# One score product per head and chunk, transposes on VectorE, and y on feature partitions in a gated linear recurrence with a dense block

## The chip, the cores and the metric

The kernel runs on one core of a Trainium2 chip. The metric is the device time of one execution in microseconds. The names used: PE is TensorE, DVE is VectorE, ACT is ScalarE, POOL is GpSimd, SP is SyncE, whose queue issues every DMA here.

## The reference

Inputs q, k, v and alpha have the shape 4 x 8 x 768 x 48 (batch, heads, tokens, features); q, k and v are normal numbers times 0.1, alpha is uniform between 0.8 and 1. The two weight matrices are float64, 384 x 2048 and 2048 x 384. What is computed:

```python
for t in range(S):
    state = alpha[:, :, t, :, None] * state + np.einsum('bhd,bhe->bhde', k[:, :, t], v[:, :, t])
    y[:, :, t] = np.einsum('bhd,bhde->bhe', q[:, :, t], state)
x = y.transpose(0, 2, 1, 3).reshape(B * S, H * D)      # 3072 x 384
h = x @ w_in
out = (h - np.tanh(h)) @ w_out                         # 3072 x 384
```

## The kernel before

The 3072 tokens are cut into 12 units of 256 tokens, a unit into two chunks of 128 (`CU`), three units to a batch entry. A unit goes through a recurrence (`gla`, lines 165 to 280) and a dense part (`moe`, lines 282 to 331). All arithmetic is fp32, and an fp32 matmul leaves two records in the trace (a transpose leaves one).

The recurrence. `load` fetches alpha, k, q and v with tokens on the partitions, two DMAs each per unit. `flip` (line 182) turns alpha, k and q round on PE, four 128 x 128 transposes per chunk and input, two heads in one (a head takes 64 partitions, 48 of them filled); the copies out of PSUM give `pre`, `kT` and `qT`. The scores of a chunk are built in seven levels of halving (line 204): at each level DVE multiplies q and k by products of alpha from and to the middle of a block (lines 209 and 213), PE makes 16 products of 64 rows, 128 columns of weights and 64 columns (line 220), DVE copies what a mask keeps into `scores` (line 225), and POOL extends the products of alpha (lines 234 and 235). The term of s = t is a row sum on POOL and DVE (lines 197 to 200). Then per chunk: y on token partitions from the state and from scores times v (lines 246 and 249), the sum with the diagonal term (253), three transposes that put features on the partitions (256), and, but for the last chunk of a batch entry, the update of the state through a transpose of k (265), a product (269) and POOL and DVE (278 and 279).

The dense part has eight steps (`FS`). `first` makes a PSUM tile of two 128-feature blocks by 256 tokens (line 292, 6 products), then four passes on ACT (square, tanh, a square of a polynomial, an overrun mask; lines 301 to 304) and six on DVE (305 to 310) that give g; where h h passes 0.25, h - tanh(h) is taken instead of the polynomial. `second` multiplies g by w_out (line 317, 4 products), two steps after its `first`.

The weights come as 28 blocks of float64 bits and are made fp32 by six passes on DVE, two on ACT and one on POOL (lines 124 to 135), through two buffers of `raw`. The temporary tiles of that conversion and of the dense passes share the tags u, z, t and w.

The order in which work is handed out is written at the end: the recurrence of a unit starts five steps before the dense part of the unit ahead of it, its 12 pieces spread over nine steps, its loads four steps earlier, and the weights before unit 0. Within that order a scheduler places each engine's instructions by their data. Each engine then runs in order.

Of the kernel before, what the change touches and what calls it, by code (L numbers as in the profile page):

```python
# [8 lines left out]
FP32 = mybir.dt.float32  # L9
# [17 lines left out]
ZK = C2 - ZB * ZB  # L27


@with_exitstack  # L30
def kernel(
# [12 lines left out]
    HD = H * D  # L44
    NP = H // 2
    G = CU * NP
    TU = CU * P
    UPB = S // TU
    NCH = S // P
    NU = B * UPB  # L50
    LEVELS = 7
    d_model, d_ff = moe_w_in.shape
    KT = d_model // P
    FT = d_ff // P
    FS = FT // 2

    w_in_r = moe_w_in.rearrange("(j p) f -> p j f", p=P)
    w_out_r = moe_w_out.rearrange("(j p) n -> p j n", p=P)
    out_r = out.rearrange("(t p) n -> t p n", p=P)

    consts = ctx.enter_context(tc.tile_pool(name="consts", bufs=1))
    two = ctx.enter_context(tc.tile_pool(name="two", bufs=2))
    three = ctx.enter_context(tc.tile_pool(name="three", bufs=3))
    ps_sc = ctx.enter_context(tc.tile_pool(name="ps_sc", bufs=2, space=PSUM))
    ps_tp = ctx.enter_context(tc.tile_pool(name="ps_tp", bufs=1, space=PSUM))
    ps_y = ctx.enter_context(tc.tile_pool(name="ps_y", bufs=1, space=PSUM))
    ps_h = ctx.enter_context(tc.tile_pool(name="ps_h", bufs=2, space=PSUM))
    ps_o = ctx.enter_context(tc.tile_pool(name="ps_o", bufs=1, space=PSUM))

    V, A, T, GP = nc.vector, nc.scalar, nc.tensor, nc.gpsimd  # L70

    ident = consts.tile([P, P], FP32, name="ident")
    make_identity(nc, ident)
    z_bias = consts.tile([P, 1], FP32, name="z_bias")
    V.memset(z_bias, ZB)
    m_bias = consts.tile([P, 1], FP32, name="m_bias")
    V.memset(m_bias, -U_MAX)
# [3 lines left out]
    mask = consts.tile([P, LEVELS, P // 2], FP32, name="mask")  # L81
    GP.memset(mask, 1.0)
    for l in range(LEVELS):
        L = 1 << l
        m = mask[:, l, :].rearrange("p (n j) -> p n j", j=L)
        n = P // (2 * L)
        GP.affine_select(out=m, in_=m, compare_op=ALU.is_ge, fill=0.0, base=0,
                         pattern=[[-2 * L, n], [0, L]], channel_multiplier=1)
        GP.affine_select(out=m, in_=m, compare_op=ALU.is_ge, fill=0.0, base=L - 1,
                         pattern=[[2 * L, n], [0, L]], channel_multiplier=-1)  # L90
# [3 lines left out]
    nat = [[consts.tile([P, CU, H, HP], FP32, name=f"{n}{i}") for n in ("an", "kn", "qn")]  # L94
           for i in range(2)]
    for i in range(2):
        for t in nat[i]:
            GP.memset(t[:, :, :, D:], 0.0)
    scores = [consts.tile([P, 2, G, P], FP32, name=f"scores{i}") for i in range(2)]
    for t in scores:  # L100
        V.memset(t, 0.0)
    states = [consts.tile([P, NP, 2 * D], FP32, name=f"state{i}") for i in range(2)]
    for t in states:
        GP.memset(t, 0.0)
# [4 lines left out]
    def load_w(dst, src):  # L109
        """A part of a weight matrix, of up to 512 columns: from float64 rounded to fp32, with  # L110
        what fp32 has no normal number for as 0 or infinite."""
        if moe_w_in.dtype == FP32:
            nc.sync.dma_start(out=dst, in_=src)
            return
        n = dst.shape[-1]
        raw = two.tile([P, 512], I64, name="raw")
        nc.sync.dma_start(out=raw[:, 0:n], in_=src)
        words = raw.bitcast(I32).rearrange("p (n w) -> p n w", w=2)
        lo, hi = words[:, 0:n, 0].bitcast(mybir.dt.uint32), words[:, 0:n, 1]
        e = two.tile([P, 512], I32, name="e", tag="u")[:, 0:n]  # L120
        m = two.tile([P, 512], I32, name="m", tag="z")[:, 0:n]
        low = two.tile([P, 512], FP32, name="low", tag="t")[:, 0:n]
        man = two.tile([P, 512], FP32, name="man", tag="w")[:, 0:n]
        V.tensor_scalar(out=e, in0=hi, scalar1=20, scalar2=0x7FF,  # L124
                        op0=ALU.logical_shift_right, op1=ALU.bitwise_and)
        V.tensor_scalar(out=e, in0=e, scalar1=896, scalar2=1151, op0=ALU.max, op1=ALU.min)
        V.tensor_scalar(out=e, in0=e, scalar1=23, scalar2=0x3FFFFFFF,  # L127
                        op0=ALU.logical_shift_left, op1=ALU.bitwise_and)
# [8 lines left out]
    def weights():  # L137
        """In the order in which the first unit needs them."""
        w = 512
        for i in range(d_ff // w):  # L140
            for j in range(KT):
                load_w(w_in[:, j, i * w:(i + 1) * w], w_in_r[:, j, i * w:(i + 1) * w])
# [236 lines left out]
```

## Time and profile before

| what | value |
|---|---|
| median of 3 runs | 1134.95 us (1134.72 to 1138.42) |
| profiled execution, span | 1140.3 us, 14741 instructions |
| PE busy | 1045.0 us, 92% |
| DVE busy | 805.0 us, 71% |
| ACT busy | 320.6 us, 28% |
| POOL busy | 342.8 us, 30% |
| mean granted PE clock | 0.909 |

The profile gives no other time for the profiled execution than its span, from the first to the last instruction; it is 5.4 us over the median of the runs. Busy times overlap between engines. [...]

### The profile page before, as it was taken

To read this page: it belongs to the slowest core of one execution; us is meant where nothing else is said; L and a number is where in the kernel's file an instruction comes from. 1 tells how busy PE (TensorE), PEld (TensorE's weight loads), DVE (VectorE), ACT (ScalarE), POOL (GpSimd) and SP (SyncE) were. 2 spreads that over 40 slices of the span, in tenths; PEclk is the share of its full clock that TensorE was granted. 3 is DMA by queue.
4 is the path that set the end of the run, shared out by engine and by line. 5 is a ranking of instruction groups with operands and counts; after the bars stand their busy time and mean duration, and the time that the engine had idled before them with its cause. 6 is when DMAs were issued, how large, how long until landed. Compare 5 with 4: busy or idle time off the path is not lost.

```text
span 1140.3 us, 14741 instructions
## 1 busy us (share of the span) xinstructions
PE 1045.0 (92%) x5752; PEld 845.6 (74%) x5752; DVE 805.0 (71%) x1212; ACT 320.6 (28%) x569; POOL 342.8 (30%) x293
## 2 busy tenths in 40 slices
PE   3765648999999999999999999999999999999988
PEld 2764548877877878778777788778787788777765
DVE  6688896584684677776774777685775676776766
ACT  2012330321421331421511431521502322413433
POOL 6454443043042044043132043143132152141000
PEclk9999755887998899989988999998979999989999
DMA  9433620110110020110200110200200000000000
GB/s 175 81 91 97 150 73 1 27 30 14 27 31 14 1 56 15 29 28 15 56 1 15 35 23 14 50 8 14 56 1 15 1 1 15 1 1 15 1 14 14
DMA packets 107396, 37.11 MB, mean 33 GB/s; under 512 B 100672, under 2 KB 103744, under 8 KB 107328
## 3 DMA queue, kind: packets, MB, share of 16 engines
q1 hardware_dynamic: 107328, 36.19, 14.1%
q8 instruction: 45, 0.74, 0.3%
q14 instruction: 23, 0.19, 0.1%
HBM read 31.46 MB, written 4.72 MB: 32 GB/s over the span
## 4 chain that ended last, share of the span: by engine, by line
PE 79%; DVE 15%; POOL 2%; issue 2%; ACT 1%; DMA 0%; SPq 0%; POOLq 0%; DVEq 0%
PE sc L220 24%; PE h L292 24%; PE o L317 20%; PE y L249 4%; DVE scores L225 3%; PE tp L185 2%; PE y L246 2%; PE up L269 2%; DVE e L129 1%; DVE W L209 1%; DVE z L307 1%; DVE e L127 1%; PE tp L265 1%; DVE m L131 1%; DVE e L124 1%
## 5 line engine op out<-in xcount | busy, mean ns | idle before, releaser
L220 PEld LDWEIGHTS sc<-W 64*128 64x128 f32 x2688 | 324.9, 217 | 92.7 <-issue 68.7
L220 PE MATMUL sc<-W 64*128 64x64 f32 x2688 | 338.1, 305 | 53.6 <-DVE W L213 41.0
L292 PE MATMUL h<-xT,w_in 128*128 128x256 f32 x1152 | 325.1, 426 | 5.1 <-DVE g L310 3.8
L317 PE MATMUL o<-w_out,g 128*128 128x384 f32 x768 | 278.7, 504 | 0.2 <-DVE g L310 0.2
L292 PEld LDWEIGHTS h<-xT,w_in 128*128 128x128 f32 x1152 | 231.7, 213 | 46.0 <-issue 4.8
L225 DVE COPY_PREDICATED scores<-mask,sc 128x512 f32<-128x512 int32 x168 | 147.8, 882 | 117.4 <-PE sc L220 115.1
L317 PEld LDWEIGHTS o<-w_out,g 128*128 128x128 f32 x768 | 147.5, 198 | 84.0 <-issue 7.7
L301 ACT ACTIVATE sq<-h 128x512 f32<-128x512 f32 x96 | 57.4, 598 | 440.9 <-PE h L292 437.1
L235 POOL TENSOR_TENSOR pre<-pre 128x512 f32<-128x512 f32 x84 | 118.3, 1409 | 115.5 <-DVE W L209 112.3
L234 POOL TENSOR_TENSOR suf<-suf,pre 128x512 f32<-128x512 f32 x72 | 100.3, 1393 | 140.3 <-DVE W L213 137.5
L305 DVE TENSOR_TENSOR w<-h,sq 128x512 f32<-128x512 f32 x96 | 66.2, 690 | 93.1 <-ACT th L302 92.4
L209 DVE TENSOR_TENSOR W<-qT,pre 128x512 f32<-128x512 f32 x84 | 60.1, 716 | 24.9 <-POOL pre L235 14.9
L310 DVE COPY_PREDICATED g<-large,h 128x512 f32<-128x512 int32 x96 | 70.6, 736 | 3.3
L309 DVE SCALAR_TENSOR_TENSOR g<-z,w 128x512 f32<-128x512 f32 x96 | 70.8, 737 | 1.8
L307 DVE SCALAR_TENSOR_TENSOR z<-z,sq 128x512 f32<-128x512 f32 x96 | 70.2, 731 | 0.0
L303 ACT ACTIVATE z<-sq,z_bias 128x512 f32<-128x512 f32 x96 | 69.6, 725 | 0.0
L304 ACT ACTIVATE large<-sq,m_bias 128x512 f32<-128x512 f32 x96 | 69.3, 722 | 0.0
L308 DVE SCALAR_TENSOR_TENSOR z<-z,sq 128x512 f32<-128x512 f32 x96 | 67.7, 705 | 1.9
L306 DVE TENSOR_TENSOR h<-h,th 128x512 f32<-128x512 f32 x96 | 66.7, 695 | 0.0
L213 DVE TENSOR_TENSOR W<-kT,suf 128x512 f32<-128x512 f32 x72 | 56.4, 784 | 14.2 <-POOL suf L234 14.2
L278 POOL TENSOR_TENSOR state<-state,pre 64x192 f32<-64x192 f32 x32 | 23.1, 722 | 139.3 <-DVE state L279 69.8
L249 PE MATMUL y<-vt,scores 128*128 128x48 f32 x384 | 53.2, 291 | 4.7 <-DVE scores L225 4.7
(60 smaller groups left out, 737.1 us busy)
## 6 DMA issues: line engine op xcount, KB each, us to landing
raw<-in_moe_w_in_dram SPq DMA_DIRECT2D x12, 512.0 KB, 3.9
raw<-in_moe_w_out_dram SPq DMA_DIRECT2D x16, 384.0 KB, 3.1
an<-in_alpha_dram SPq DMA_DIRECT2D x24, 192.0 KB, 3.3
kn<-in_k_dram SPq DMA_DIRECT2D x24, 192.0 KB, 3.5
qn<-in_q_dram SPq DMA_DIRECT2D x24, 192.0 KB, 3.1
vt<-in_v_dram SPq DMA_DIRECT2D x24, 192.0 KB, 3.9
out_dram<-ob SPq DMA_DIRECT2D x24, 192.0 KB, 1.9
```

Of the source, the lines that this page charges most:

```text
L209: V.tensor_mul(W1, q1, p1)
L220: T.matmul(sc[:, g, :], lhsT=Wf[rows, g, :], rhs=Wh[rows, g, :, 1, :], start=True, stop=True)
L225: V.copy_predicated(out=to, mask=on.unsqueeze(1).to_broadcast([P, G, n, L]), data=sc.rearrange("p g (n j) -> p g n j", j=L))
L234: GP.tensor_mul(s0, s0, e1)
L235: GP.tensor_mul(p1, p1, e0)
L249: T.matmul(y[:, h * D:(h + 1) * D], lhsT=P_[:, h % 2, c * NP + h // 2, :], rhs=vt[:, c, h, :], start=(n == 0 and h == 0), stop=True, skip_ ...
L292: T.matmul(h[:, a, :], lhsT=w_in[:, j, f * P:(f + 1) * P], rhs=x_t[:, j, :], start=(j == 0), stop=(j == KT - 1))
L303: A.activation(z, sq, AF.Square, bias=z_bias, scale=ZA)
L307: V.scalar_tensor_tensor(out=z, in0=z, scalar=ZK, in1=sq, op0=ALU.add, op1=ALU.mult)
L309: V.scalar_tensor_tensor(out=g, in0=z, scalar=C0, in1=w, op0=ALU.add, op1=ALU.mult)
L310: V.copy_predicated(out=g, mask=large.bitcast(I32), data=h)
L317: T.matmul(o[c], lhsT=g[:, a * TU + c * P:a * TU + (c + 1) * P], rhs=w_out[:, f, :], start=(f == 0), stop=(f == FT - 1))
```

## The change

The old recurrence and its dense part become a function `general`, with single buffers, placed behind a flag. A new function `fast` runs first. Its parts:

- Inputs: q, k and alpha are loaded as 32 partitions of 8 tokens by 48 features for each pair of heads, twice with a shift of 32 features, and turned by three 32 x 32 block transposes on DVE, without PE.
- Scores: with U the product of alpha from a token to the chunk's end and 1/ends the inverse of the whole chunk's product, scans on DVE make U and the scaled running product, POOL multiplies k and q by them, and one product per head and chunk gives all scores, masked by one DVE product. The diagonal is part of it.
- y comes with features on the partitions; ACT copies it into x, and small DMAs move the last pair's features into the 16-row gaps that each block of 128 partitions has. The rows of w_in are loaded in the same order.
- Dense: the polynomial is a product of two squares (two ACT squares, three DVE passes); the overrun is only summed.
- At the end one flag is made from the sums (no h h over 0.25, no scaled product over 2^60, no chunk product under 2^-60), read by the engines, and `general` runs where it is 0.

```diff
+        def load(u):
+            b, i = divmod(u, UPB)
+            t0 = i * TU
+            for t, x in zip(raws[u % 2], (alpha, k, q)):
+                for hh in range(2):
+                    src = x[b].rearrange("(g two) s d -> two g (s d)", two=2)[hh][:, t0 * D:(t0 + TU) * D]
+                    src = src.rearrange("g (i n) -> i g n", i=32)
+                    for dq in range(2):
+                        at = 64 * hh + 32 * dq
+                        nc.sync.dma_start(
+                            out=t[at:at + 32].rearrange("p g r d -> p g (r d)")[:, :, 0:R * D - 32 * dq],
+                            in_=src[:, :, 32 * dq:])
...
+            for t, raw in zip((aT, kT, qT), raws[u % 2]):
+                V.transpose(t.rearrange("p g c t -> p g (c t)").rearrange("p g (i r) -> p g r i", r=R),
+                            raw[:, :, :, 0:32])
+                yield
...
+            for c in range(CU):
+                for g in range(NP):
+                    V.tensor_tensor_scan(out=U[:, g, c, P - 2::-1], data0=aT[:, g, c, P - 1:0:-1],
+                                         data1=aT[:, g, c, P - 1:0:-1], initial=1.0,
+                                         op0=ALU.mult, op1=ALU.bypass)
+            V.tensor_mul(ends, U[:, :, :, 0], aT[:, :, :, 0])
+            V.tensor_reduce(out=least[:, u:u + 1], in_=ends, axis=AX.XY, op=ALU.min)
+            V.tensor_single_scalar(out=ends, in_=ends, scalar=1.0 / R_MAX, op=ALU.max)
+            V.reciprocal(inv, ends)
+            yield
+            for c in range(CU):
+                for g in range(NP):
+                    V.tensor_tensor_scan(out=aT[:, g, c, :], data0=aT[:, g, c, :],
+                                         data1=aT[:, g, c, :], initial=inv[:, g, c:c + 1],
+                                         op0=ALU.mult, op1=ALU.bypass)
+            GP.tensor_mul(kT, kT, U)
+            GP.tensor_mul(qT, qT, aT)
+            for n, t in enumerate((U, aT)):
+                junk = two.tile([P, NP * TU], FP32, name="junk", bufs=1)
+                A.activation(junk, t.rearrange("p g c t -> p (g c t)"), AF.Square,
+                             accum_out=sizes[:, 2 * u + n:2 * u + n + 1])
...
+                for g in range(NP):
+                    for hh in range(2):
+                        at = slice(HP * hh, HP * hh + D)
+                        T.matmul(sc[hh][:, g, :], lhsT=kT[at, g, c, :], rhs=qT[at, g, c, :],
+                                 start=True, stop=True)
+                for hh in range(2):
+                    V.tensor_mul(pm[hh], sc[hh], mask.unsqueeze(1).to_broadcast([P, NP, P]))
...
+                        GP.tensor_mul(old[at], old[at], ends[at[0], :, c:c + 1].to_broadcast([D, NP, D]))
...
+                        T.matmul(y[0:EV, g, :], lhsT=old[:, g, :], rhs=qT[:, g, c, :],
+                                 start=(g == 0), stop=False, skip_group_check=True)
+                for g in range(NP):
+                    for hh in range(2):
+                        T.matmul(y[HP * hh:HP * hh + D, g, :], lhsT=vt[:, c, 2 * g + hh, :],
+                                 rhs=pm[hh][:, g, :], start=(n == 0 and g == 0), stop=True,
+                                 skip_group_check=True)
...
+                for hh in range(2):
+                    at = slice(HP * hh, HP * hh + D)
+                    A.copy(xs[at], y[at, NP - 1, :])
+                    A.copy(x_t[at, :, to], y[at, 0:KT, :])
+                for j in range(KT):
+                    for at, f0 in pad_rows[j][2:]:
...
+                        nc.sync.dma_start(out=x_t[at, j, to], in_=xs[r0:r0 + at.stop - at.start])
...
+                A.activation(sq, h, AF.Square)
+                A.activation(z1, sq, AF.Square, bias=QB1, scale=QA)
+                A.activation(z2, sq, AF.Square, bias=QB2, scale=QA)
+                V.tensor_mul(w, h, sq)
+                V.scalar_tensor_tensor(out=z1, in0=z1, scalar=QK1, in1=w, op0=ALU.add, op1=ALU.mult)
+                V.scalar_tensor_tensor(out=g, in0=z2, scalar=QK2, in1=z1, op0=ALU.add, op1=ALU.mult)
+                n = u * FS + s
+                A.activation(big, sq, AF.Relu, bias=-U_MAX, accum_out=over[:, n:n + 1])
...
+        MOE, GLA, EARLY = FS + 1, 5 + 3 * CU, 5.0
...
+        row = ps_y.tile([P, P], FP32, name="row", tag="tp")
+        T.transpose(row[0:1, :], fine[:, 0:1], ident)
+        V.tensor_reduce(out=ok, in_=row[0:1, :], axis=AX.X, op=ALU.min)
...
+    fast(tc, q, k, v, alpha, moe_w_in, moe_w_out, out, w_in, w_out, ident, ok, pad_rows)
+    with tc.If(nc.values_load(ok[0:1, 0:1], min_val=0, max_val=1) < 1):
+        general(tc, q, k, v, alpha, w_in, w_out, out, ident, pad_rows)
```

The order written at the end is the same one, with a recurrence in 11 pieces instead of 12. The tags of the weight conversion are u, z1, z2 and w. The score tiles in PSUM have one buffer for each half, y one, the transposed k and the update share one.

## Rows read from the trace of the kernel before

**Rows 1.** Busy times, part 1 of the page: busy us (share) xinstructions.

```profile
PE 1045.0 (92%) x5752; PEld 845.6 (74%) x5752; DVE 805.0 (71%) x1212; ACT 320.6 (28%) x569; POOL 342.8 (30%) x293
```

**Rows 2.** The chain that ended last, by line, part 4 of the page.

```profile
PE sc L220 24%; PE h L292 24%; PE o L317 20%; PE y L249 4%; DVE scores L225 3%; PE tp L185 2%; PE y L246 2%; PE up L269 2%; DVE e L129 1%; DVE W L209 1%; DVE z L307 1%; DVE e L127 1%; PE tp L265 1%; DVE m L131 1%; DVE e L124 1%
```

**Rows 3.** Busy us (x instructions) of PE, PEld, DVE, ACT, POOL by stage; clock, DMA.

```profile
150.00:200.00 50.00, 33.12 (x172) 32.52 (x173) 38.36 (x66) 9.22 (x17) 20.16 (x17) 0.50 0.11 32
276.00:1033.00 757.00, 749.25 (x4321) 600.26 (x4319) 526.01 (x779) 216.14 (x385) 222.64 (x175) 0.93 0.09 20
340.00:348.00 8.00, 8.00 (x32) 6.93 (x32) 2.95 (x6) 0.00 (x0) 0.00 (x0) 0.50 0.00 0
```

**Rows 4.** The copies of results, by tile: ns min/median/max, first and last start (us).

```profile
L329 ACT COPY ob<-o x24: 479/479/482, 276.2 to 1136.8; 128x384 f32<-128x384 f32 x24
```

**Rows 5.** PE's timeline in unit 1: start us, us, operation, xrecords.

```profile
298.03 2.74 PE L317 MATMUL o<-w_out,g 128*128 128x384 f32 x8
300.61 1.03 PE L246 MATMUL y<-state,qT 128*128 128x96 f32 x8
301.48 1.91 PE L249 MATMUL y<-vt,scores 128*128 128x48 f32 x16
303.23 1.53 PE L292 MATMUL h<-xT,w_in 128*128 128x256 f32 x6
...
319.99 3.39 PE L220 MATMUL sc<-W 64*128 64x64 f32 x32
323.31 2.20 PE L317 MATMUL o<-w_out,g 128*128 128x384 f32 x6
...
343.29 3.67 PE L220 MATMUL sc<-W 64*128 64x64 f32 x16
```

**Rows 6.** PE's timeline in the last unit.

```profile
1098.21 4.23 PE L292 MATMUL h<-xT,w_in 128*128 128x256 f32 x12 [3.82 <-DVE g L310]
...
1105.15 2.75 PE L292 MATMUL h<-xT,w_in 128*128 128x256 f32 x12
1107.74 2.74 PE L317 MATMUL o<-w_out,g 128*128 128x384 f32 x8
```

**Rows 7.** Groups by line: operation xcount | busy us, mean ns | idle before, releaser.

```profile
L235 POOL TENSOR_TENSOR pre<-pre 128x512 f32<-128x512 f32 x84 | 118.3, 1409 | 115.5 <-DVE W L209 112.3
L309 DVE SCALAR_TENSOR_TENSOR g<-z,w 128x512 f32<-128x512 f32 x96 | 70.8, 737 | 1.8
L303 ACT ACTIVATE z<-sq,z_bias 128x512 f32<-128x512 f32 x96 | 69.6, 725 | 0.0
L305 DVE TENSOR_TENSOR w<-h,sq 128x512 f32<-128x512 f32 x96 | 66.2, 690 | 93.1 <-ACT th L302 92.4
L301 ACT ACTIVATE sq<-h 128x512 f32<-128x512 f32 x96 | 57.4, 598 | 440.9 <-PE h L292 437.1 <-DVE w_out L135 3.8
L278 POOL TENSOR_TENSOR state<-state,pre 64x192 f32<-64x192 f32 x32 | 23.1, 722 | 139.3 <-DVE state L279 69.8 <-DVE state L275 68.2
L186 DVE COPY pre<-tp 128x512 f32<-128x512 f32 x24 | 16.5, 686 | 2.5 <-PE tp L185 2.2
L279 DVE TENSOR_TENSOR state<-state,up 64x192 f32<-64x192 f32 x32 | 11.1, 348 | 1.2 <-PE up L269 0.4 <-PE h L292 0.3
```

**Rows 8.** Tile e alone, first 180 us: DVE busy us (x instructions), clock, DMA.

```profile
0.00:180.00 180.00, 88.48 (x140) 0.85 0.46 105
```

**Rows 9.** Tile m alone, the same stretch: DVE and ACT busy us.

```profile
0.00:180.00 180.00, 15.59 (x28) 15.97 (x28) 0.85 0.46 105
```

**Rows 10.** ACT's timeline where the dense passes begin in earnest.

```profile
174.45 0.60 ACT L301 ACTIVATE sq<-h 128x512 f32<-128x512 f32 x1 [3.81 <-DVE w_out L135]
```

**Rows 11.** Tile raw: ns min/median/max, first and last start (us); landing of its DMAs.

```profile
L124 DVE TENSOR_SCALAR e<-raw x28: 345/416/1697, 13.7 to 168.2; 128x384 int32<-128x384 int32 x16, 128x512 int32<-128x512 int32 x12
...
L117 SPq DMA_DIRECT2D raw<-in_moe_w_in_dram x12: 327/340/1111, 7.9 to 141.4; - x12
...
DMA to landing us min/median/max: 2.8/3.4/5.2
```

More of the change, by code (lines that the diff above doesn't have):

```diff
@@ L70 @@
-    V, A, T, GP = nc.vector, nc.scalar, nc.tensor, nc.gpsimd
+    d_model, d_ff = moe_w_in.shape
+    KT, FT = d_model // P, d_ff // P
+    gap = HP - D
+    pad_rows = []
+    for j in range(KT):
+        last = (H - 2) * D
+        pad_rows.append([(slice(0, D), 2 * j * D), (slice(HP, HP + D), (2 * j + 1) * D),
+                         (slice(D, HP), last + j * gap),
+                         (slice(HP + D, P), last + D + j * gap)])
+    consts = ctx.enter_context(tc.tile_pool(name="consts", bufs=1))
@@ L72 @@
     ident = consts.tile([P, P], FP32, name="ident")
     make_identity(nc, ident)
[L74 to L90, printed above, removed]
@@ L94 @@
[L94 to L104, printed above, removed]
     w_in = consts.tile([P, KT, d_ff], FP32, name="w_in")
@@ L107 @@
     w_out = consts.tile([P, FT, d_model], FP32, name="w_out")
[L109 to L128, printed above, removed]
-        V.scalar_tensor_tensor(out=e, in0=hi, scalar=-0x40000000, in1=e,
-                               op0=ALU.bitwise_and, op1=ALU.bitwise_or)
-        V.tensor_single_scalar(out=m, in_=hi, scalar=0xFFFFF, op=ALU.bitwise_and)
-        A.activation(man, m, AF.Copy, bias=1.0, scale=2.0 ** -20)
-        A.activation(low, lo, AF.Copy, scale=2.0 ** -52)
-        GP.tensor_add(man, man, low)
-        V.tensor_mul(dst, man, e.bitcast(FP32))
@@ L137, in weights @@
[L137 to L142, printed above, removed]
-            yield
-            for f in range(i * w // P, (i + 1) * w // P):
-                load_w(w_out[:, f, :], w_out_r[:, f, :])
-            yield
-    loaded = {}
-    def load(u):
-        b, i = divmod(u, UPB)
-        vt = three.tile([P, CU, H, D], FP32, name="vt")
-        for c in range(CU):
-            t0 = i * TU + c * P
-            def rows(x):
-                return x[b, :, t0:t0 + P, :].rearrange("h p d -> p h d")
-            for t, x in zip(nat[u % 2], (alpha, k, q)):
-                nc.sync.dma_start(out=t[:, c, :, 0:D], in_=rows(x))
-            nc.sync.dma_start(out=vt[:, c], in_=rows(v))
-        loaded[u] = vt
@@ L335 @@
-    MOE, GLA, EARLY = FS + 1, 1 + LEVELS + 2 * CU, 5.0
-    order = []
-    for u in range(NU):
-        order += [(u * MOE + i, 1, "moe", u) for i in range(MOE)]
-        at = (u - 1) * MOE - EARLY
-        order += [(at + i * MOE / GLA, 0, "gla", u) for i in range(GLA)]
-        order += [(at - 4, 0, "load", u)]
-    order += [(-MOE - EARLY + 2 + i, 2, "weights", 0) for i in range(2 * d_ff // 512)]
-    make = {"moe": moe, "gla": gla, "load": load, "weights": lambda _: weights()}
-    live = {}
@@ L345 @@
-    for _, _, what, u in sorted(order):
-        if (what, u) not in live:
-            live[what, u] = make[what](u) or iter(())
-        next(live[what, u], None)
+    ok = consts.tile([1, 1], I32, name="ok")
+    fast(tc, q, k, v, alpha, moe_w_in, moe_w_out, out, w_in, w_out, ident, ok, pad_rows)
+    with tc.If(nc.values_load(ok[0:1, 0:1], min_val=0, max_val=1) < 1):
+        general(tc, q, k, v, alpha, w_in, w_out, out, ident, pad_rows)
 _INS = ['q', 'k', 'v', 'alpha', 'moe_w_in', 'moe_w_out']
```

532 lines of the change are left out of this document (358 added, 174 removed).

## The prediction

> **What bounds the kernel now.** Read the busy times first: TensorE (PE) is busy for 1045.0 us, 92% of the span of 1140.3 us [rows 1]. A busy PE need not be the limit, so the chain that ended last comes second: it runs through the score products (line 220) for 24% of the span, the two dense products (292 and 317) for 24% and 20%, and VectorE's lines for a few per cent each [rows 2]. The views by stage come third. The out copies give the boundaries: unit 0 ends at 276.2 us, the last one at 1136.8 [rows 4]. Between 276 and 1033 us nine units end, 84.1 us each; there PE is busy for 749 of 757 us, VectorE (DVE) for 526, ScalarE (ACT) for 216 and GpSimd (POOL) for 223 [rows 3]. So the middle is PE-bound. [...]
>
> PE's pace comes from starts in its timeline at full clock. Eight records (an fp32 product leaves two) of the second dense product take 300.61 - 298.03 = 2.58 us, 322 ns each; of the state product 301.48 - 300.61 over 8, 109 ns; of scores times v 303.23 - 301.48 over 16, 109 ns; 32 of the score products 323.31 - 319.99, 104 ns [rows 5]. The first dense product takes 1107.74 - 1105.15 over 12, 216 ns [rows 6]. Per unit, at full clock: dense 96 x 0.216 + 64 x 0.322 = 41.4 us; scores 224 x 0.104 = 23.3; the other 102 records (32 transposes of inputs and k, 6 of x, 48 for y, 16 for the update, all taken at 0.11) 11.2. Sum 75.9 against 84.1 measured: the factor is 1.108, of which a mean clock of 0.93 explains 1.075 [rows 3].
>
> **The change, part by part.**
> Scores: seven levels x 16 products become 16 products of 128 columns, 32 records. A record of 128 columns is not in the trace for 48 rows; the bounds are the score record (104 ns) and half a dense one of 256 columns (108), so I take 0.11: 3.5 us, 19.8 less per unit.
> Transposes: 24 of the inputs and 6 of x leave PE, 3.3 us less. The 8 of k stay. y turns round (features on the partitions): its 48 records have 128 columns instead of 48 or 96, still near 0.11. PE per unit is 41.4 + 104 records x 0.11 = 52.8 us, 23.1 less.
> DVE: six dense passes become three, 8 x (0.690 + 2 x 0.737) = 17.3 us per unit [rows 7]. Seven levels of products and masked copies go. New are three block transposes of 1024 elements a partition, by the copy of 512 at 0.686 [rows 7] 1.4 us each, at worst twice that; and 16 scans of 128 elements, between 0.1 and 0.69 (the copy, four times as long), of which I take 0.3 because the 192-element add at 0.348 is the nearest row [rows 7]. With four mask products (0.69), four state adds (0.35) and five small ones (0.1) the recurrence costs 4.2 + 4.8 + 2.8 + 1.4 + 0.5 = 13.7 us, DVE 31 per unit, at worst 41. That is under 52.8, so nothing of it stands on the path in the middle.
> ACT: three squares and the sum of overruns instead of four passes: 8 x (0.598 + 3 x 0.725) = 22.2, with copies and two long squares some 31 us. POOL: two products of 1024 elements (twice 1.41 each) and four state products (0.72) [rows 7], 8.5 us against 223 / 9 = 24.7. Both have cover from PE; if it went, ACT would be next, still 20 us away.
> SP: a unit issues 28 DMAs (12 for the inputs, 2 for v, 12 that move padding rows of x, 2 out) instead of 10, at 0.34 each 9.5 us [rows 11]. The padding DMAs wait for a copy of y, and the loads of the next unit and the results queue behind them. They land in about 3.4 us [rows 11] and are handed in 6.6 steps (over 30 us) before the dense part reads x, so I cost them at nothing. Without that lead each unit would wait some 5 us.
> Weights: the same conversion, in padded row order, with 48 DMAs instead of 12 for w_in (12 us more of issues on SP, spread over 120).
>
> **The first 140 us.** The dense elementwise work shares tags (u, z, w) with the weight conversion, and the first square that had to wait for it starts at 174.45, released by the last weight product [rows 10]. On DVE the conversion costs 88.5 (tile e) and 15.6 (tile m) us [rows 8, 9]. The same pass takes from 345 to 1697 ns [rows 11], the long ones beside GpSimd. A recurrence costs DVE 526 / 9 less 34.4 of dense passes = 24 us. Before: 13.7 (first pass [rows 11]) + 104 + 24 for unit 0 and some 20 for unit 1 = 162, and 12 of waits, mostly on scores. After: POOL's load falls to a third, so I take 95 for the conversion, 13.7 + 12 for the recurrences, and 4 of waits: 138. [...] Unit 0 ends at 198 instead of 276. Bounds: 167 (conversion at 83, half of the rest hidden) and 232 (conversion not faster).
>
> **The sum.** Nine units at 52.8 x a factor. Without loss 1.00, with today's 1.108; I take 1.04, because half-clock stretches come among score products (340 to 348 us: PE busy for all 8.00 us at 0.50 [rows 3], 16 records in 3.67 us instead of 1.7 [rows 5]), and those shrink from 23.3 to 3.5 us. So 55 each, 495 in all. Unit 10 carries half a recurrence: 48. The last unit is dense only: today's 46 with its wait of 3.82 us and 4.23 us for a first step that later takes 2.6 [rows 6]; I leave it at 46.
> The end: a reduction of flags, a value read by the engines, and a branch past the general block. No row has a branch; the nearest bounds are 0.3 us (a short pass) and some 15 us (four dependent DMA landings of 3.4); I take 6, near two landings.
> 198 + 495 + 48 + 46 + 6 = 793 us, against the profiled 1140.3. The runs' median is 1134.95, 0.5% under that execution, so the forecast is **788**.
> [...]
>
> **Rivals.**
> 1. Row and column halves run side by side. The new score products alternate between partitions 0 to 47 and 64 to 111, and y alternates between output halves; today 16 products in a row use the same half, at 104 ns. If pairs overlapped, 64 records would cost half: 64 x 0.055 = 3.5 us per unit over 11 units, 39 less: **750**. [...] Against it: no row shows two records overlapping. [...]
> 2. Waits take the place of the work. DVE runs in order, and the chain of transposes, scans, products on POOL, scores, mask and y is longer per link than a level was. If PE idles once a unit and its clock falls as in 340 to 348, some 7 us per unit come back: 62 each, **855**. For it: today's factor of 1.108. Against: PE waits only 8 us in 757 at a DVE load of 526, and that falls to 9 x 31 = 280.
> 3. The start does not shorten: two raw buffers and quartered DMAs, not DVE, pace the conversion. Unit 0 ends at 235: **825**.
> 4. Slower: the flag fails and the general block runs behind the fast one. Its place is the end. Its price is at least one more pass over all units at today's pace, 788 + 1135 = **1920**, more since it is single-buffered. It decides when any |h| passes 0.5 (h h over 0.25), or a product of alpha over a chunk falls under 2^-60. The reference's inputs give at most 0.091 and at least 8.3e-8 (2^-60 is 8.7e-19), so only a flag that does not say what it means could do it.
> The change not doing what it says is that case too.
>
> **How the numbers follow.** Forecast 0.50 (its own range 760 to 820), rival 1 0.15, rival 2 0.19, rival 3 0.12, rival 4 0.04. The range 735 to 862 holds the first, the third and most of the second and fourth of these cases; it leaves out the flag, units slower than 62 us, and a start near 167 together with overlapping halves. What a measurement can tell from no change is 0.3%, 3.4 us; none of the fast cases comes near: faster 0.95, same 0.01, slower 0.04.
>
> **What would show it.** Right: unit ends about 55 us apart from the second on, PE busy over 97% between, records of line sc at about 110 ns, DVE near 31 us per unit, the first square after the weights near 138 us, unit 0 out near 198, and under 10 us between the last out copy and the end. Wrong: PE waits released by POOL or by scans (rival 2), records in pairs at 55 ns (rival 1), ACT or DVE waiting for raw DMAs (rival 3). Over 1000 us the reading that PE binds would be wrong altogether.

## The result: 788.6 us, ratio 0.694

The changed kernel takes 788.6 us (median of 4 runs, 785.88 to 792.79) against 1135.12 (1134.72 to 1138.42) for the one before: a ratio of 0.694, 95% interval 0.691 to 0.697. The forecast was 788, and it holds. But that it meets 788.6 so closely is luck: two terms of the sum behind it are off by some 24 and 32 us with opposite signs, and the total hides that. Two runs reported below, one of 798.32 us (no branch) and one of 767.25 us (three buffers, tags, padding), were in a slower state of the chip: they are in the medians and ranges given but not in the ratios.

The profiled execution has a span of 783.7 us, with 3089 PE records instead of 5752. Busy times, part 1 of the page after, answering to [rows 1]:

```profile
PE 627.0 (80%) x3089; PEld 462.9 (59%) x3089; DVE 477.8 (61%) x828; ACT 336.7 (43%) x725; POOL 118.2 (15%) x110
```

PE's share fell from 92% to 80%, so it looks less bound. The stages say otherwise. The result copies give the unit ends, as in [rows 4] (tile ob after: ns min/median/max, first and last start):

```profile
L474 ACT COPY ob<-o x24: 479/479/480, 221.2 to 776.2; 128x384 f32<-128x384 f32 x24
```

Unit 0 is out at 221.7 us, the tenth unit after it at 734.7, which is 51.3 us each (over nine units, as in the prediction, 51.4 against 84.1 before), and 7.5 us lie between the start of the last copy and the end. The stretches, answering to [rows 3] (same columns: length, then PE, PEld, DVE, ACT and POOL busy, the granted clock of PE as a share of the full one and a mean over the stretch, DMA share, GB/s):

```profile
0.00:50.00 50.00, 15.78 (x80) 12.93 (x80) 21.52 (x42) 8.30 (x15) 11.41 (x24) 1.00 0.41 85
50.00:100.00 50.00, 4.74 (x28) 3.55 (x26) 41.15 (x78) 14.56 (x28) 14.86 (x13) 1.00 0.58 135
100.00:150.00 50.00, 16.99 (x119) 13.80 (x118) 39.72 (x87) 15.84 (x32) 14.48 (x15) 0.69 0.47 116
150.00:180.00 30.00, 1.12 (x4) 0.72 (x4) 24.00 (x47) 11.16 (x21) 10.42 (x8) 0.50 0.58 135
...
222.00:735.00 513.00, 508.64 (x2566) 374.82 (x2565) 301.41 (x500) 247.37 (x548) 61.28 (x49) 1.00 0.24 53
```

From 222 to 735 us PE is busy 99% of the time at full clock. Nearly all the idle time of PE is in the first 180 us, of which it works 39. Nor is DVE saturated there: 126 of 180 us, the first 50 of them least.

PE's pace, from its timeline after (start, us, line, operation, records), answering to [rows 5]:

```profile
221.73 1.16 PE L382 MATMUL sc<-qT,kT 48*128 48x128 f32 x16
222.82 1.13 PE L394 MATMUL y<-qT,state 128*112 128x128 f32 x8
223.78 1.03 PE L442 MATMUL h<-xT,w_in 128*128 128x256 f32 x4
...
239.04 1.08 PE L398 MATMUL y<-pm,vt 128*48 128x128 f32 x16
240.05 2.86 PE L442 MATMUL h<-xT,w_in 128*128 128x256 f32 x12
...
245.32 2.75 PE L442 MATMUL h<-xT,w_in 128*128 128x256 f32 x12
247.91 2.74 PE L462 MATMUL o<-w_out,g 128*128 128x384 f32 x8
250.49 2.75 PE L442 MATMUL h<-xT,w_in 128*128 128x256 f32 x12
```

A score record takes (222.82 - 221.73) / 16 = 68 ns and a record of masked scores times v (240.05 - 239.04) / 16 = 63 ns; a state record (223.78 - 222.82) / 8 = 120. The dense records are as before: 216 and 322 ns. The trace holds 97 records a unit beside the 160 dense ones (2566 / 10 in the last row above), since the last chunk of a batch entry has no update and the first no state product: 32 of scores, 13.3 of state products, 32 of scores times v and 20 of transposes and updates. At these prices, with 0.11 for the last 20, a unit is 41.4 us of dense products, 2.2 of scores, 1.6 and 2.0 of y, 2.2 of transposes and updates: 49.4, against 51.3 measured.

At the start DVE's timeline shows how it loses time (in brackets: idle before, and what ended it):

```profile
11.55 0.69 DVE L66 TENSOR_TENSOR w_in<-man,e 128x512 f32<-128x512 f32 x1 [1.54 <-POOL man L65]
12.16 2.01 DVE L344 STREAM_TRANSPOSE aT<-ar 128x1024 f32<-128x1024 f32 x1
14.21 2.61 DVE L351 TENSOR_TENSOR_SCAN U<-aT 128x127 f32<-128x127 f32 x8
...
17.70 3.11 DVE L361 TENSOR_TENSOR_SCAN aT<-aT,inv 128x128 f32<-128x128 f32 x8
20.72 2.01 DVE L344 STREAM_TRANSPOSE kT<-kr 128x1024 f32<-128x1024 f32 x1
29.12 0.74 DVE L427 COPY state<-up 48x192 f32<-48x192 f32 x2 [6.39 <-PE up L422]
33.91 0.74 DVE L429 TENSOR_TENSOR state<-state,up 48x192 f32<-48x192 f32 x2 [4.04 <-PE up L422]
34.67 2.02 DVE L344 STREAM_TRANSPOSE qT<-qr 128x1024 f32<-128x1024 f32 x1
41.34 1.29 DVE L385 TENSOR_TENSOR pm<-sc,mask 128x512 f32<-128x512 f32 x2 [4.65 <-PE sc L382]
42.55 0.42 DVE L55 TENSOR_SCALAR e<-raw 128x512 int32<-128x512 int32 x1
...
173.17 0.56 DVE L66 TENSOR_TENSOR w_out<-man,e 128x384 f32<-128x384 f32 x1 [1.19 <-POOL man L65]
173.65 2.02 DVE L344 STREAM_TRANSPOSE kT<-kr 128x1024 f32<-128x1024 f32 x1
```

One of 28 weight blocks is converted by 12 us; the second begins at 42.55, behind all of unit 0's recurrence on DVE but its last two mask products, and the links of that chain run over POOL, PE and ACT. The conversion therefore ends late. The last weight product but one starts at 173.17, and behind it come the first dense square, on ACT's timeline at 174.48 and so just where it was before [rows 10], and unit 2's block transpose of k. For that PE, in its own order, has stood 61 us (PE's timeline after):

```profile
178.39 1.12 PE L418 MATMUL tp<-ident,kT 128*128 128x128 f32 x4 [61.40 <-POOL kT L364]
```

That is the longest of three such waits, which are most of PE's idle time in the first 180 us (PE's waits after: us, times, longest):

```profile
PE tp L418 <- POOL kT L364: 131.3, 3, 61.4
```

Unit 0 is out 55 us sooner than before (its first copy starts at 221.2, where it was 276.2), though its dense steps begin no sooner: from the first square on it took 276.2 - 174.45 = 102 us before and takes 47 now.

### The profile page after: what moved, and what is told of

Same layout as the page of the kernel before. It is cut to its first block, busy times and chain, and to the rows that moved or that the text cites. A ratio compares the mean times of both kernels' runs of the same rounds, so it can differ in the third digit from the quotient of the medians.

```text
span 783.7 us, 9136 instructions
## 1 busy us (share of the span) xinstructions
PE 627.0 (80%) x3089; PEld 462.9 (59%) x3089; DVE 477.8 (61%) x828; ACT 336.7 (43%) x725; POOL 118.2 (15%) x110
## 5 line engine op out<-in xcount | busy, mean ns | idle before, releaser
L442 PE MATMUL h<-xT,w_in 128*128 128x256 f32 x1152 | 277.7, 387 | 0.9 <-DVE w L451 0.9
L451 DVE TENSOR_TENSOR w<-h,u 128x512 f32<-128x512 f32 x96 | 66.0, 687 | 157.6 <-ACT u L448 157.3
L448 ACT ACTIVATE u<-h 128x512 f32<-128x512 f32 x96 | 57.2, 596 | 162.6 <-PE h L442 162.1
L418 PE MATMUL tp<-ident,kT 128*128 128x128 f32 x80 | 14.1, 305 | 132.2 <-POOL kT L364 131.3
L452 DVE SCALAR_TENSOR_TENSOR z<-z,w 128x512 f32<-128x512 f32 x96 | 71.8, 747 | 9.7 <-ACT z L449 2.8
L453 DVE SCALAR_TENSOR_TENSOR g<-z,z 128x512 f32<-128x512 f32 x96 | 66.1, 688 | 6.4
L385 DVE TENSOR_TENSOR pm<-sc,mask 128x512 f32<-128x512 f32 x48 | 31.9, 685 | 60.3 <-PE sc L382 60.3
L449 ACT ACTIVATE z<-u 128x512 f32<-128x512 f32 x96 | 60.6, 631 | 2.7
L455 ACT ACTIVATE big<-u 128x512 f32<-128x512 f32 x96 | 59.1, 615 | 0.0
L450 ACT ACTIVATE z<-u 128x512 f32<-128x512 f32 x96 | 59.0, 615 | 0.0
L361 DVE TENSOR_TENSOR_SCAN aT<-aT,inv 128x128 f32<-128x128 f32 x96 | 44.8, 510 | 0.2
L351 DVE TENSOR_TENSOR_SCAN U<-aT 128x127 f32<-128x127 f32 x96 | 34.6, 423 | 4.0 <-POOL kT L364 3.8
```

The costliest lines, as they stand in the source:

```text
L351: V.tensor_tensor_scan(out=U[:, g, c, P - 2::-1], data0=aT[:, g, c, P - 1:0:-1], data1=aT[:, g, c, P - 1:0:-1], initial=1.0, op0=ALU.mult, ...
L361: V.tensor_tensor_scan(out=aT[:, g, c, :], data0=aT[:, g, c, :], data1=aT[:, g, c, :], initial=inv[:, g, c:c + 1], op0=ALU.mult, op1=ALU.b ...
L385: V.tensor_mul(pm[hh], sc[hh], mask.unsqueeze(1).to_broadcast([P, NP, P]))
L442: T.matmul(h[:, a, :], lhsT=w_in[:, j, f * P:(f + 1) * P], rhs=x_t[:, j, :], start=(j == 0), stop=(j == KT - 1))
L448: A.activation(sq, h, AF.Square)
L449: A.activation(z1, sq, AF.Square, bias=QB1, scale=QA)
```

## The experiments

Ratios below stand against the kernel before, run beside them (medians 1139 to 1143 us); "after" is the changed kernel. A unit's time is the mean over the ten units that follow unit 0.

### Product order: one half at a time

```diff
-                for g in range(NP):
-                    for hh in range(2):
+                for hh in range(2):
+                    for g in range(NP):
```

(for the score products, and again for scores times v)

> The score products and the products for y are handed out with all heads of one partition half first, then those of the other, instead of alternating. Theory A (alternating halves run side by side on PE: 68 and 72 ns a record in the changed kernel against 104 to 110 in the one before): in a row of one half each record costs about 107 ns again, 64 records a unit, 2.4 us a unit, 28 us in all: about 816 us. Theory B (the records are short because they load 48 rows or 48 columns of weights): the order does not matter, 788 within 5.

Measured: 803.37 us (801.84 to 804.85), ratio 0.704 [0.700, 0.709]; a unit takes 52.8 us, 1.5 more than after. PE's timeline of this kernel:

```profile
327.00 1.71 PE L382 MATMUL sc<-qT,kT 48*128 48x128 f32 x16
328.64 1.13 PE L394 MATMUL y<-qT,state 128*112 128x128 f32 x8
329.70 1.55 PE L398 MATMUL y<-pm,vt 128*48 128x128 f32 x16
331.19 2.86 PE L442 MATMUL h<-xT,w_in 128*128 128x256 f32 x12
```

The same products now take 1.64 / 16 = 102 ns and 1.49 / 16 = 93 ns. So records that alternate between the halves follow each other a third closer than records of one half, not twice as close (68 ns, where half of 102 is 51), and 803 lies between the two theories (816, and 788 within 5). What overlaps, two products or one's weight load with the other's product, these rows do not tell; the score products also alternate between two PSUM tiles, but those for y do not and gain as much. By the rows 64 records a unit differ by (102 - 68) x 32 + (93 - 63) x 32 = 2.0 us; 1.5 is what the unit shows.

### The old dense passes in the new kernel

```diff
-                A.activation(z1, sq, AF.Square, bias=QB1, scale=QA)
-                A.activation(z2, sq, AF.Square, bias=QB2, scale=QA)
+                A.activation(th, h, AF.Tanh)
+                A.activation(z, sq, AF.Square, bias=ZB, scale=ZA)
...
+                V.tensor_sub(h, h, th)
+                V.scalar_tensor_tensor(out=z, in0=z, scalar=ZK, in1=sq, op0=ALU.add, op1=ALU.mult)
...
+                V.copy_predicated(out=g, mask=big.bitcast(I32), data=h)
```

(two more passes of DVE and the mask pass on ACT are not shown here; the overrun is not summed)

> The changed kernel with the dense passes of before (four on ACT, six on DVE; the sum of overruns is left out). DVE then has 34.4 + 17.5 = 52 us a unit against 50.5 on PE. Theory A (DVE becomes the bound, so the shorter polynomial is needed to harvest the shorter PE work): 53 to 58 us a unit, 815 to 870 us in all. Theory B (PE still sets the pace as it did in the kernel before): no more than 795.

Measured: 845.14 us (844.59 to 848.29), ratio 0.741 [0.736, 0.746]. Unit 0 ends 12 us later (233.7) and a unit takes 55.7 us, 4.4 more. The middle by stage, and what PE waits for in it (us, times, longest):

```profile
234.00:790.00 556.00, 519.84 (x2548) 379.28 (x2547) 446.56 (x739) 229.19 (x467) 57.80 (x48) 0.99 0.21 47
```

```profile
PE h L443 <- DVE g L459: 26.9, 23, 4.6
PE o L466 <- DVE g L459: 5.6, 3, 2.9
```

The time is theory A's. Its reason holds in part: with six passes DVE is busy 44.7 us of 55.7 in each unit and not the 52 expected, so PE waits for it though DVE has time left. The shorter polynomial is needed once PE's unit has shrunk to 51 us: it is worth 57 us here, 12 of them before unit 0 is out.

### The shorter polynomial in the kernel before

```diff
-            A.activation(th, h, AF.Tanh)
-            A.activation(z, sq, AF.Square, bias=z_bias, scale=ZA)
+            A.activation(z, sq, AF.Square, bias=z_bias, scale=QA)
+            A.activation(z2, sq, AF.Square, bias=z2_bias, scale=QA)
...
+            V.scalar_tensor_tensor(out=z, in0=z, scalar=QK1, in1=w, op0=ALU.add, op1=ALU.mult)
+            V.scalar_tensor_tensor(out=g, in0=z2, scalar=QK2, in1=z, op0=ALU.add, op1=ALU.mult)
```

(the three other passes of DVE go; the overrun is not acted on)

> The kernel before with the shorter polynomial alone (two squares and an overrun pass on ACT, three passes on DVE; the overrun is not acted on). Theory A (PE binds in the middle, the dense passes lie beside it): 1120 to 1135 us, all of the gain in the first 280 us. Theory B (DVE runs in order, and the levels of the scores wait there behind dense passes, which holds PE and its clock down): under 1095 us.

Measured: 1160.18 us (1152.33 to 1163.92), ratio 1.013 [1.005, 1.022]. That is 0.5 to 2.2% longer, not clearly beyond 2%, and neither theory allowed it: both expected a gain. The middle of this kernel, and six microseconds inside a run of score products:

```profile
273.00:881.00 608.00, 607.88 (x3351) 489.74 (x3350) 318.33 (x437) 180.64 (x298) 169.52 (x135) 0.87 0.11 23
686.00:692.00 6.00, 6.00 (x40) 6.00 (x38) 2.15 (x4) 0.00 (x0) 0.00 (x0) 0.53 0.00 0
```

DVE fell from 58 to 45 us a unit and PE's waits are gone: 607.88 of 608 us busy. But the mean clock is 0.87 instead of 0.93 [rows 3], so a unit takes 86.9 us over the seven units of this window (87.0 over nine, where 84.1 stood); 86.9 x 0.87 = 75.6, near the 75.9 us of records that the prediction counted. What the old kernel lost in the middle was therefore mostly clock and not waits, and in this pair of kernels the one that waits less has the lower clock. The six microseconds lie in 64 score records on end, where [rows 5] has runs of 16 and 32; that the longer runs lower the clock is a reading that this run does not isolate.

### More score products in the new kernel

```diff
+                for hh in range(2):
+                    at = slice(HP * hh, HP * hh + D)
+                    for i in range(24):
+                        T.matmul(sc[hh][:, i % NP, 0:64], lhsT=kT[at, i % NP, c, :], rhs=qT[at, i % NP, c, 0:64],
+                                 start=True, stop=True)
```

> The changed kernel, but each chunk first makes 48 extra score products (24 in a row on each row half, 64 columns), whose results the real ones overwrite: 192 more records a unit, as many of the old kind as the kernel before has more. At 104 ns that is 20.0 us a unit at full clock. Theory A (runs of half-array score products are what lowers PE's granted clock, with no wait of PE): the mean clock of the middle falls under 0.95 though PE stays busy, a unit takes 76 us or more, the time is 1050 us or more. Theory B (the clock was low for another reason, of the old kernel's elementwise work or its waits): clock 1.00, 51.3 + 20.0 = 71.3 us a unit, 785.9 + 11 x 20.0 = about 1006 us.

Measured: 1220.76 us (1220.07 to 1224.21), ratio 1.073 [1.069, 1.077]; a unit takes 89.6 us. The middle as a whole, then three stretches of one chunk's score products, then a dense one:

```profile
273.70:1169.50 895.80, 895.72 (x4539) 745.51 (x4538) 303.35 (x508) 251.59 (x552) 58.53 (x48) 0.79 0.14 30
...
364.70:369.70 5.00, 5.00 (x47) 5.00 (x46) 0.00 (x0) 0.48 (x1) 0.00 (x0) 1.00 0.83 199
369.70:374.00 4.30, 4.30 (x29) 4.30 (x28) 0.00 (x0) 0.00 (x0) 0.00 (x0) 0.57 0.48 88
374.00:378.50 4.50, 4.50 (x23) 4.50 (x23) 0.00 (x0) 0.00 (x0) 0.00 (x0) 0.50 0.00 0
381.40:390.00 8.60, 8.60 (x38) 5.84 (x38) 1.58 (x3) 2.52 (x7) 0.00 (x0) 0.65 0.01 3
410.00:450.00 40.00, 40.00 (x167) 29.38 (x167) 24.77 (x41) 17.17 (x37) 6.21 (x4) 0.94 0.29 63
```

Theory A holds, by far more than it asked, and a busy PE alone is not the cause: after, PE is busy 99% of the middle at 1.00. PE never idles, and the granted clock falls from 1.00 to 0.50 inside the run of small products (106 ns a record, then 4.50 / 23 = 196) and comes back among the dense products behind it (0.94 from 410 to 450 us). At full clock 192 records would cost 20 us a unit by the prediction's 104 ns; the unit grew by 38.3, of which nearly half is clock: 89.6 x 0.79 = 70.8, as theory B's 71.3 would have it at 1.00. What property of these products it is (48 rows, 64 columns, a weight load to each) no run here separates.

### Transposes back on TensorE

```diff
-                V.transpose(t.rearrange("p g c t -> p g (c t)").rearrange("p g (i r) -> p g r i", r=R),
-                            raw[:, :, :, 0:32])
+                for c in range(CU):
...
+                        T.transpose(tp[:, g, :], raw[:, c, 2 * g:2 * g + 2, :], ident)
+                    copy(t[:, :, c, :], tp)
```

(and loads with tokens on the partitions)

> The changed kernel with alpha, k and q loaded with tokens on the partitions and turned by PE (24 transposes a unit, copies on DVE and ACT) as before. Theory A (PE binds, so each of its records counts at 0.11 us): 2.6 us a unit, 31 in all, about 818 us. Theory B (what PE loses DVE gains, 6.1 us a unit of block transposes, above all in the first 200 us where DVE binds): 790 to 800.

Measured: 829.33 us (826.42 to 830.06), ratio 0.725 [0.720, 0.730]. Unit 0 is 18 us earlier (204.1), a unit takes 57.5 us, 6.2 more. The middle by stage, and its largest wait:

```profile
204.00:779.00 575.00, 544.58 (x2709) 398.34 (x2708) 275.63 (x486) 265.80 (x580) 61.08 (x48) 0.96 0.13 28
```

```profile
PE tf L342 <- ACT qT L343: 29.0, 8, 4.2
```

Theory B's gain came at the start, but the middle lost more than it, and the total lies above both theories. 24 records at 0.11 are 2.6 us of the 6.2. 2.9 are waits for the copies out of PSUM, and a clock of 0.96 goes with them; the loads changed too, and no run separates them. The edit cost more than the records of its transposes.

### No branch at the end

```diff
-    with tc.If(nc.values_load(ok[0:1, 0:1], min_val=0, max_val=1) < 1):
-        general(tc, q, k, v, alpha, w_in, w_out, out, ident, pad_rows)
```

> The read of the flag and the branch with the general block are left out (the flag is still computed). Theory A: from the last copy of results to the end the changed kernel takes 7.5 us, the one before 3.5; the branch is the difference, 4 us, about 784 us. Theory B: the end is the landing of the results in both, and the branch costs nothing: 788.

Measured: 785.96 us (779.85 to 798.32), ratio 0.686 [0.680, 0.693]. The medians don't tell it from after, since the runs spread by more than the effect. The profiled executions do: last copy at 780.5 and span 783.7, 3.2 us, against 7.5 after. (Both spans are 783.7 us because unit 0 came out 3.3 us later in this execution, which no run explains.) So the value read and the branch take about 4.3 us together, near theory A's 4; no run tells the two apart.

### The start: order, buffers, tags

Six kernels change what happens before unit 0 is out; only the moved padding DMAs and the tag of `big` act in later units too.

```diff
-        order += [(-MOE - EARLY + 2 + i, 2, "weights", 0) ...
+        order += [(-MOE - EARLY - 4.5 + i, 2, "weights", 0) ...
```

> The weight blocks are handed out ahead of unit 0's loads and recurrence, so that three blocks are converted before DVE comes to unit 0's transposes and the next ones between its steps. Theory A (the start is long because DVE, in order, sits behind unit 0's chain: busy 21.5 of the first 50 us with one of 28 blocks done): about 25 us of waits are filled, unit 0 ends near 200 instead of 222, 765 to 770 us. Theory B (the two raw buffers and the landing of their DMAs pace the conversion, 5.1 us a block over 139 us): the 27 blocks left keep that pace, unit 0 gains at most 10 us, 778 or more.

```diff
-    raw = pool.tile([P, 512], I64, name="raw")
+    raw = pool.tile([P, 512], I64, name="raw", bufs=4)
```

> The changed kernel with four buffers for the raw weight blocks instead of two. Theory A (waits of DVE behind unit 0's chain make the start long): no more than 6 us less, 782 or more. Theory B (the raw buffers pace the conversion: DVE and ACT waited 16 and 27 us for raw DMAs): unit 0 ends 15 to 25 us earlier, 765 to 773.

Both edits of these two together:

> Weight blocks ahead of unit 0's recurrence and four raw buffers together. If both waits are real and separate, their gains add: 745 to 765 us. If one hides the other, it is no better than the better of the two alone.

Three raw buffers, and the conversion's tiles under tags of their own:

```diff
-    e = pool.tile([P, 512], I32, name="e", tag="u")[:, 0:n]
+    e = pool.tile([P, 512], I32, name="e", tag="we")[:, 0:n]
...
-                big = two.tile([P, 2 * TU], FP32, name="big", bufs=1)
+                big = two.tile([P, NP * TU], FP32, name="big", tag="junk", bufs=1)[:, 0:2 * TU]
```

(m, low and man likewise; big gives the room)

> The changed kernel with three raw buffers and temporary tiles of the conversion that share no tag with the dense passes. Theory A (the dense squares of unit 0 still wait for the last weight product through the shared tags): unit 0 ends near 188 us instead of 199.9 with four raw buffers alone, time near 750. Theory B (what is late next is PE in its order, behind unit 1's recurrence): no more than the four buffers gave, 758 to 766 us.

Four raw buffers, the padding DMAs on another queue:

```diff
-                        nc.sync.dma_start(out=x_t[at, j, to], ...
+                        nc.scalar.dma_start(out=x_t[at, j, to], ...
```

> Four raw buffers, and the DMAs that move padding rows of x are issued from ScalarE's queue instead of SyncE's, where they stand behind the loads of the weights. Theory A (PE's 9.9 us of waits on those DMAs at the start are on the path): unit 0 ends near 190 us instead of 199.9, time near 752. Theory B (they lie beside another wait): 758 to 766 us. [...]

The padding DMAs moved and the tags apart, with three raw buffers:

> Three raw buffers, the conversion's tiles under tags of their own, and the padding DMAs on ScalarE's queue. If both of the two edits take time off the path of unit 0: 735 to 750 us, unit 0 out near 180. If one hides the other: the better of the two alone. If PE's order behind unit 1's recurrence binds: 758 to 766 us.

| kernel | us (runs) | ratio | unit 0 out | unit 2 out |
|---|---|---|---|---|
| after | 788.6 (785.9 to 792.8) | 0.694 [0.691, 0.697] | 221.7 | 321.7 |
| weights ahead | 762.8 (762.5 to 763.3) | 0.668 [0.664, 0.672] | 193.2 | 303.2 |
| four raw buffers | 761.5 (760.6 to 762.6) | 0.667 [0.662, 0.671] | 199.9 | 300.7 |
| both | 767.4 (763.8 to 770.0) | 0.671 [0.666, 0.676] | 195.8 | 308.6 |
| three, own tags | 757.6 (755.0 to 760.1) | 0.665 [0.662, 0.667] | 184.0 | 301.4 |
| four, padding moved | 769.2 (767.8 to 770.3) | 0.675 [0.673, 0.678] | 207.6 | 308.8 |
| three, tags, padding | 754.3 (753.2 to 767.3) | 0.662 [0.659, 0.666] | 193.1 | 291.6 |

The first row of the stage with the weights ahead shows the cure at work, DVE busy 38 of the first 50 us instead of 21.5:

```profile
0.00:50.00 50.00, 16.71 (x96) 13.92 (x96) 37.99 (x70) 14.31 (x28) 16.00 (x28) 1.00 0.60 133
```

Four raw buffers reach nearly the same time by the other side: the first 50 us are as after (DVE 21.5), and the conversion behind them no longer waits for its loads (DVE's waits for tile raw fall from 16.1 us to the 7.7 of the very first load). So theory A holds for the order and theory B for the buffers, each 2 to 4 us beyond the range it gave. With both, the conversion's first pass of the last block starts at 119.2, where it was 175.5 after (tile e in both kernels, ns min/median/max, first and last start):

```profile
L55 DVE TENSOR_SCALAR e<-raw x28: 344/355/931, 6.0 to 119.2; 128x384 int32<-128x384 int32 x16, 128x512 int32<-128x512 int32 x12
```

```profile
L55 DVE TENSOR_SCALAR e<-raw x28: 334/418/996, 7.7 to 175.5; 128x384 int32<-128x384 int32 x16, 128x512 int32<-128x512 int32 x12
```

That is 56 us sooner, and worth nothing over either alone: the first square comes at 149.69, where the weights ahead alone have it at 149.45. PE's waits of that kernel in the first 200 us say why (us, times, longest):

```profile
PE tp L418 <- POOL kT L364: 112.7, 2, 81.1
```

PE runs in order, and here it stands 81 us in front of unit 1's transpose of k, with unit 0's dense products queued behind it. That transpose needs POOL's product of the k which DVE turns round at 132.62, behind the whole conversion (DVE's timeline of that kernel):

```profile
123.25 0.56 DVE L66 TENSOR_TENSOR w_out<-man,e 128x384 f32<-128x384 f32 x1
123.72 2.01 DVE L344 STREAM_TRANSPOSE aT<-ar 128x1024 f32<-128x1024 f32 x1
...
132.62 2.00 DVE L344 STREAM_TRANSPOSE kT<-kr 128x1024 f32<-128x1024 f32 x1
```

What was unit 0's recurrence in front of the weights is now the weights in front of unit 1's recurrence, so the gains of the two edits don't add, as the second of the two expectations had it.

Tags of the conversion's own let the first square start at 132.99, beside the conversion (ACT's timeline of that kernel):

```profile
132.99 0.60 ACT L448 ACTIVATE u<-h 128x512 f32<-128x512 f32 x1
```

Unit 0 is out at 184.0, 16 us before the four buffers alone, but units 1 and 2 then take 61.0 and 56.5 us, and unit 2 is out no earlier (301.4 against 300.7). The stages of these two units (184 to 245 and 245 to 301 us) show clocks below 1.00 and 6.5 and 3.5 us in which PE is idle:

```profile
184.00:245.00 61.00, 54.50 (x255) 40.24 (x254) 43.97 (x69) 26.42 (x57) 10.39 (x6) 0.92 0.34 71
245.00:301.00 56.00, 52.47 (x256) 38.13 (x256) 42.55 (x68) 25.27 (x56) 9.68 (x7) 0.95 0.37 77
```

The head start is given back; that the next recurrences have less lead then is a reading of these rows, which no run tests. The total of 757.6 lies between the two theories' figures (750, and 758 to 766); half right is the fair reading.

Moving the padding DMAs alone missed: 769.2 where 752 or 758 to 766 was expected. PE's waits for those DMAs fell only from 9.9 to 5.9 us, while one wait for DVE in front of a dense product grew from 24.9 to 41.9 (PE's waits of this kernel, first 210 us):

```profile
PE h L442 <- DVE w L451: 41.9, 1, 41.9
...
PE h L442 <- DMA xT<-xs: 5.9, 1, 5.9
```

The move has a price of its own. On ScalarE's queue each of these DMAs takes 0.6 us to issue, 12 of them 7.2 us a unit, and behind unit 0 dense squares wait for them 16 times, 46.2 us in all, with PE as cover: a unit takes 51.2 us (the DMAs of that kernel: ns min/median/max, first and last start):

```profile
L411 ACTq DMA_DIRECT2D xT<-xs x144: 514/600/1511, 46.2 to 691.6; - x144
```

The first square starts at 163.01 instead of 160.03 with four buffers alone, and unit 0 is out 7.7 us later. What made it later no run separates.

Together with the tags it gives the shortest median, 754.3, 34 us under after and ratio 0.662 [0.659, 0.666]; from the tags alone its interval does not part it. Unit 0 is out 9 us later than with the tags alone (193.1, where 180 was expected if both edits helped), so of the three expectations "the better of the two alone" fits best.

## Why the prediction was right, and where its terms were not

| term | forecast | measured | difference |
|---|---|---|---|
| unit 0 out | 198 | 221.7 | +23.7 |
| nine units | 495 | 462.9 | -32.1 |
| unit 10 | 48 | 50.1 | +2.1 |
| last unit | 46 | 41.5 | -4.5 |
| end | 6 | 7.5 | +1.5 |
| sum | 793 | 783.7 | -9.3 |

The last step was luck too. The sum of 793 was lowered by 0.5%, because the profiled execution before was longer than the median of the runs. After, the profiled one is the fastest of the four, 783.7 us of span against a median of 788.6, so the step went the other way and made up for the 9.3.

**The reading that PE binds the middle: right.** It is busy for 99% of it, before and after, and the time per unit follows its records and their clock. "PE busy over 97%", "DVE near 31 us per unit" (301.41 / 10 = 30.1) and "under 10 us between the last out copy and the end" came out. Rivals 2 and 4 did not occur: in the middle no engine's wait took the place of the work, and the general block did not run. The sign named for rival 2, PE waits released by POOL, does show, but at the start alone (131.3 us).

**The pace of the records: mis-sized, rival 1 in good part true.** The prediction took 0.11 for each of 104 records, 11.4 us a unit; by the rows there are 97 of them and they take 8.0. Over nine units, with the factor, the count is some 7 us of the 32 and the pace some 25. Products in turn on the two halves cost 68 and 63 ns, not 110 and not 55. Undoing the order returns 15 us of the 39 which the rival had; the rest of the pace is that even in a row of one half they take 102 and 93. The argument against the rival, that no row showed two records overlapping, was true of the trace and said nothing on a case that the trace did not have.

**The factor 1.04: its size right, its reason right and more so.** By the 97 records it is 51.4 / 49.4 = 1.04. The prediction put the lost clock down to the score products, because rows of half clock lay among them with PE fully busy [rows 3, 5], and expected it to shrink with them. It did not shrink but went: the clock of the middle is 1.00, and of the 4% that are left 0.9 are PE's waits (508.64 of 513 us busy) and the rest no row isolates. The run with more score products shows that such products can take it, a clock of 0.79 without a wait of PE, and the run with the short polynomial alone agrees, with fewer waits and a lower clock. By this reading the seven levels cost more than their 19.8 us a unit.

**The start: the step that failed.** DVE's work was rightly sized: tiles e and m take 75.28 and 12.76 us in the first 180 us, 88 against the 95 allowed, answering to [rows 8, 9], and up to the first square DVE works for 120.9 us in all, against 95 + 13.7 + 12 = 120.7. What was wrong is its idle time: 13.7 us before the first pass and "4 us of waits" were allowed, and it was idle for 53.6, so "the first square after the weights near 138 us" came at 174.48. The 198 allows unit 0 another 60 us behind that square, which no run shows: it took 47 (174.48 to 221.7, at a mean clock of 0.90), which is why its end is off by 24 and not by 36. The prediction counted DVE's work as if it had no order. It runs in one: the weights of unit 0 are handed out behind the first recurrence, whose steps now pass through POOL, PE and ACT in turn, so each link stands in front of conversion work that could have run. Of the idle time 23 us end with a PE product of a recurrence. The loads are the second cause, and rival 3 had it: 16 us end with a load of tile raw. Another 12 end with POOL's pass inside the conversion. Either cure, the order or the buffers, takes off 26 to 27 us. Unit 0 came nearer to rival 3's 235 than to the forecast's 198; the middle made up for it. What is late next, PE's order in front of the next unit's transpose, the prediction did not name.

**New prices.** Block transposes take 2.03 us (taken: 1.4, at worst 2.8). The eight scans of either kind in a unit take 2.61 and 3.11 us, 0.33 and 0.39 each (taken: 0.3). ACT took 24.7 us a unit (31), POOL 6.1 (8.5). None of it stands on the path in the middle. The padding DMAs, costed at nothing, cost nothing from unit 1 on, where no wait of PE names them; at the start PE waits 9.9 us for them once there are four raw buffers.

**What the 346 us are.** Put back alone, the long passes cost 57 us, the transposes on PE 41, the order of halves 15. If these add, which no run tests, 233 us are left. The old score products and the clock that they took with them are argued to be most of that; they were not put back as they were. Put back in number alone, 192 records a unit, they cost 432, more than the whole gain. Their runs are of some 93 records on end against 16 to 32 in [rows 5]; that this is why they cost more clock than the old ones did is a reading, not shown.

## What to carry to other kernels

Before pricing the removal of small matmuls, look at the granted clock of their stretch: of the 38.3 us that 192 of them cost a unit here, 18 did not show in their full-clock duration. For a start-up stage, walk each engine's order and ask of every dependent chain which independent work is queued behind it; counting an engine's work gives a lower bound. And sum the terms against the trace one by one even where the total fits.

## Not expected of the hardware

- Half-array products cost 68 ns a record when the two halves alternate and 102 ns when one half follows itself (16 records, fp32, 48 rows, 128 columns); with output halves instead of row halves, 63 and 93 ns.
- A small DMA issued from ScalarE's queue holds that queue for 0.6 us (median of 144): 16 dense squares waited some 2.9 us each (46.2 in all) behind runs of them.
- With PE busy for 895.72 of 895.80 us the granted clock's mean was 0.79. A clock lost this way shows in no wait.
- A 32 x 32 block transpose of 1024 fp32 elements a partition takes 2.03 us, three times the 0.686 us of a copy of 512 and so half as much again per element (1.98 against 1.34 ns). The scan of 127 elements, from a constant, goes at 0.33 us and that of 128 elements, from a column, at 0.39; their own durations in the profile are longer (0.423 and 0.510) because they overlap. Per element a scan thus costs 2.6 to 3.0 ns (0.326 / 127 and 0.389 / 128) against the copy's 1.34 (0.686 / 512).
